# A small store of transposed maxima, issued from ScalarE's queue at some places and from SyncE's at the others

## The chip, the cores and the metric

The program runs on one core of a Trainium2 chip. Its time is the device time of one execution in microseconds (us). Three runs of the kernel before gave 2234.05, 2234.30 and 2235.77 us; the median, 2234.3 us, is the time that the prediction is held against. Beside them one execution was profiled: it took 2233.03 us, and the span of its trace, from the first to the last recorded work, is 2231.2 us. All times inside the trace count from the start of that span.

## The reference

A gated mix of two blocks over the same tokens `x` (2048 tokens of 576 values), in fp32:

```
g   = sigmoid(sum(x * gate_w))                   # one gate a token
q,k,v = split(x @ wqkv), 32 heads of 18 values
p   = softmax(q k^T / sqrt(18))                  # 2048 x 2048 a head
a   = (p v, heads side by side) @ wo
b   = gelu(layernorm(x) @ w1 + b1) @ w2 + b2     # 576 -> 4608 -> 576
out = g * a + (1 - g) * b
```

The softmax needs the maximum of each row of scores. The kernel finds these maxima in a first pass over the scores, and takes them off inside the matmul of a second pass.

## The kernel before

The attention is cut into 32 units: 16 pairs of heads (`pair`), each in two halves of 1024 queries (`unit`, L192). A unit goes through two passes.

First pass (`s1_round`, L220): 32 rounds a unit. In a round TensorE (PE) multiplies 128 queries by 512 keys for both heads (L230), and VectorE (DVE) reduces each 128x512 bank of scores to its 128 maxima (L232). When the last round of a unit is through, `s1_finish` (L234) reduces the four partial maxima, negates them, splits them in a high and a low part (L239 to L241), and transposes the 128x32 result into the tile `tr` (L244). `tr` is then stored to a scratch tensor in DRAM, `mx_scr` (16 KB, L255), and from there two small DMAs put the values as two extra rows for each head into the query tile `qa` of that unit (`rows`, L248; the DMAs are in the helper `dma_r`, L139). The second DMA waits until the store has landed; both are 8 KB.

Second pass (`s2`, L263): for each of 16 key chunks `kc` and two query blocks `qb`, PE multiplies keys by queries with the extra rows included, so that the scores come out with the maxima taken off (L271), ScalarE (ACT) takes the exponential (L274), and PE multiplies by the values (`pv`, L289). The first matmul of a unit's second pass cannot start before both rows of that unit have landed in `qa`. The first pass runs ahead of the second by about one unit.

Between the attention matmuls the kernel weaves in the MLP, piece by piece (`mlp`, L338): `h_pair` (L461) makes two chunks of the hidden layer from the normalised tokens (L490), the gelu runs on ACT (L541, L543) and GpSimd (POOL, `pool_op`, L183), and `out_pair` (L548) multiplies by `w2` (L578) and adds into an accumulator on DVE (L595). The tokens are worked in four blocks of 512. At the end of a block `h_pair` loads the next block's tokens in pieces (`load_y`, L608: `big<-y_scr`, 28 DMAs for a change of block, called from L493 and L494, issued at L139). After the MLP comes the output projection (`out_proj`, L1037; its matmuls are at L1225). Its first input is loaded by `load_o` and `load_den` (L1064, L1076: `x<-ot_scr` and `low<-ot_scr`), while the last unit is still ahead of the second pass.

The order of all this is written out when the program is built. There is a counter of slots, `slot[0]`, raised by `run_due` (L158); `defer(n, fn)` (L146) runs `fn` once n slots have gone by, so that its instructions come at that place in their engine's program. Each engine works its own program in order. DMAs issued from `nc.sync` stand in the program of SyncE (SP) in the order of the calls, and one that waits holds up those behind it. In `s1_finish` the store is deferred by 2 slots and `rows` by 7.

`inflow[0]` holds the slot of the last `load_y` or `load_o`, that is, of the last large load. The two row DMAs already go by GpSimd's queue where the loop has begun (`looped`) and that load is fewer than `BUSY` = 20 slots back, and by SP's elsewhere (L250). The store goes by SP always:

```
queue = nc.gpsimd if looped[0] and slot[0] - inflow[0] < BUSY else nc.sync
...
defer(2, lambda: nc.sync.dma_start(scr, tr))
defer(7, rows)
```

Following the slot counter through the code, the last `load_y` before the store of a unit lies 1 slot back for unit 23 (slots 1493 and 1494), the `load_o` before it lies 1 slot back for unit 31 (2005 and 2006), and for no other unit is a large load fewer than 49 slots back. The store of unit 15 stands one slot ahead of the first `load_y` of its change of block (982 and 983), its `rows` 5 slots later, among those loads.

Of the kernel before, what the change touches and what calls it, by code (L numbers as in the profile page):

```python
# [46 lines left out]
BUSY = 20  # L47
# [22 lines left out]
def gated_mix_kernel(ctx: ExitStack, tc: tile.TileContext, x, wqkv, wo, w1, b1, w2, b2, gate_w, out):  # L70
    nc = tc.nc
# [65 lines left out]
    def dma_r(queue, dst, src):  # L137

        queue.dma_start(dst.bitcast(F32), src)  # L139


    slot = [0]
    inflow = [-BUSY]
    later = []

    def defer(n, fn):  # L146
        later.append((slot[0] + n, fn))
# [86 lines left out]
    def s1_finish(u):  # L234

        m4 = M4.pop(u)
        nm = asm.tile([P, 2, 8], F32, name="nm")
        nm2 = asm.tile([P, 2, 2, 8], F32, name="nm2")
        nc.vector.tensor_reduce(nm, m4, axis=AX.X, op=ALU.max, negate=True)  # L239
        nc.vector.tensor_tensor(nm2[:, :, 0, :].bitcast(F32R), nm, nm, op=ALU.max)  # L240
        nc.vector.tensor_tensor(nm2[:, :, 1, :], nm, nm2[:, :, 0, :], op=ALU.subtract)  # L241

        tr = asm.tile([P, 32], F32, name="tr", bufs=1)
        nc.vector.transpose(tr, nm2.rearrange("p a b c -> p (a b c)"))  # L244

        scr = mx_scr[u % 2]

        def rows():  # L248
            qa = QA[u % 3]
            queue = nc.gpsimd if looped[0] and slot[0] - inflow[0] < BUSY else nc.sync  # L250
            src = scr.rearrange("(i h b t) n -> h b t i n", h=2, b=2, t=8)
            for h in range(2):
                r = 64 * h + 54
                dma_r(queue, qa[r:r + 2, :].rearrange("b (t i n) -> b t i n", i=4, n=32), src[h])
        defer(2, lambda: nc.sync.dma_start(scr, tr))  # L255
        defer(7, rows)

    RING = []
# [69 lines left out]
    looped = [False]  # L328

    def next_round():  # L330
        if rounds:
            u, r = rounds.pop()
            s1_round(u, r)
            if r == NR - 1:
                defer(1, lambda: s1_finish(u))
# [1007 lines left out]
```

## Time and profile before

| | before |
|---|---|
| median of three runs | 2234.3 us |
| the profiled execution | 2233.03 us |
| its span | 2231.2 us |
| PE busy | 2202.0 us, 99% of the span |
| DVE, ACT, POOL busy | 1647.7, 1425.7, 1006.1 us |
| moved by DMA | 329.74 MB, 148 GB/s over the span |
| stores `mx_scr<-tr` at L255, all by SP | 32 of 16 KB |
| row DMAs `qa<-mx_scr` by SP, by POOL | 58 and 6, of 8 KB |

How to read the lines shown below. A row of a timeline is: start, duration (both us), engine, source line, operation, output and input by the program's names, count of instructions merged in the row, and in brackets how long the engine had been idle and what ended that. `SPq`, `ACTq` and `POOLq` are the programs that issue DMAs; a DMA's row there is its issue, not its transfer. A row of the chain of waits, the chain of work that ended last, is: start, duration, and what the chain stood on then; a row such as `DMA mx_scr<-tr` is the time from the issue of that store to its landing, "issue" is time for which the trace shows no cause. In a table of windows the columns are the window, its length, the busy time of PE, PE's weight loads, DVE, ACT and POOL with counts, the clock granted to PE as a share of full speed, the busy share of the DMA engines, and GB/s.

### The profile page before, as it was taken

What the parts mean: (1) busy time and instruction counts of PE and PEld (TensorE: products, weight loads), DVE (VectorE), ACT (ScalarE), POOL (GpSimd) and SP (SyncE); (2) the same over time, 40 slices, a digit from 0 to 9 for tenths busy, and PEclk for the clock granted to TensorE, in tenths of its full rate; (3) what the DMA queues carried; (4) which work ended last, traced back from release to release, by engine and by line L of the source; (5) the groups of instructions that cost most, each with busy time, mean ns of one, the idle gap of its engine ahead of it and who ended that gap; (6) DMA issues with size and microseconds to landing.
All of it is one profiled execution on the core that took longest, in us unless ns stands there. A gap on an engine that the chain in (4) does not pass through costs nothing.

```text
span 2231.2 us, 51473 instructions
## 1 busy us (share of the span) xinstructions
PE 2202.0 (99%) x20496; PEld 1584.4 (71%) x20496; DVE 1647.7 (74%) x2888; ACT 1425.7 (64%) x2623; POOL 1006.1 (45%) x1003
## 2 busy tenths in 40 slices
PE   8999999999999999999999999999989999999989
PEld 7878667677766767767777677776756777776758
DVE  6685777777778777777777777777767777777634
ACT  4333777777776666666666666666656666666662
POOL 4322765666663444444445444444444444444600
PEclk9999999999999999999999999999999999999999
DMA  8867555454464533233354333232634333232354
GB/s 265 269 221 222 189 174 162 146 160 147 157 215 147 161 120 124 100 124 121 120 168 158 106 116 108 100 119 94 181 116 155 119 127 122 100 112 98 114 184 167
DMA packets 171538, 329.74 MB, mean 148 GB/s; under 512 B 65206, under 2 KB 91506, under 8 KB 160570
## 3 DMA queue, kind: packets, MB, share of 16 engines
q1 hardware_dynamic: 169138, 322.70, 44.7%
q8 instruction: 161, 2.64, 0.5%
q10 hardware_dynamic: 1968, 3.70, 0.4%
q14 instruction: 79, 0.65, 0.1%
q0 software_dynamic: 192, 0.06, 0.0%
HBM read 234.00 MB, written 96.69 MB: 148 GB/s over the span
## 4 chain that ended last, share of the span: by engine, by line
PE 94%; DVE 2%; DMA 2%; issue 1%; POOL 1%; ACT 0%; SPq 0%; DVEq 0%; ACTq 0%; POOLq 0%
PE ps L289 21%; PE ps L578 21%; PE ps L490 20%; PE ps L271 13%; PE ps L230 11%; PE ps L890 3%; PE ps L1225 3%; PE ps L911 2%; DVE m L232 1%; DMA mx_scr<-tr 1%; DMA p<-in_A_wqkv_dram 0%; PE ps L766 0%; PE ps L893 0%; PE ps L892 0%; DMA qa<-mx_scr 0%
## 5 line engine op out<-in xcount | busy, mean ns | idle before, releaser
L232 DVE TENSOR_REDUCE m<-ps 128x1 f32<-128x512 f32 x2048 | 1311.0, 684 | 390.4 <-PE ps L230 379.7
L274 ACT ACTIVATE p<-ps 128x512 f32<-128x512 f32 x1048 | 568.6, 596 | 322.5 <-PE ps L271 319.9
L274 ACT ACTIVATE ring<-ps 128x512 f32<-128x512 f32 x1000 | 543.1, 596 | 295.0 <-PE ps L271 293.2
L490 PE MATMUL ps<-big,w 64*128 64x512 f32 x3708 | 570.7, 393 | 0.2 <-issue 0.2
L183 POOL TENSOR_SCALAR zz<-zz 128x512 f32<-128x512 f32 x288 | 178.2, 619 | 736.8 <-ACT zz L543 696.2
L578 PE MATMUL ps<-w,hh 64*128 64x288 f32 x4352 | 478.7, 294 | 1.0 <-DVE x L595 1.0
L271 PE MATMUL ps<-qa,ka 56*128 56x512 f32 x2048 | 451.4, 421 | 16.8 <-DMA qa<-mx_scr 15.8
L578 PEld LDWEIGHTS ps<-w,hh 64*128 64x128 f32 x4352 | 419.1, 187 | 30.6 <-DVE x L595 5.1
L230 PE MATMUL ps<-ka,qa 54*128 54x512 f32 x2048 | 427.6, 398 | 0.1
L490 PEld LDWEIGHTS ps<-big,w 64*128 64x128 f32 x3708 | 371.8, 187 | 64.6 <-issue 0.5
L183 POOL TENSOR_TENSOR zz<-zz,z 128x512 f32<-128x512 f32 x288 | 371.4, 1290 | 24.0
L271 PEld LDWEIGHTS ps<-qa,ka 56*128 56x128 f32 x2048 | 205.7, 184 | 242.8 <-DVE m L232 173.3
L578 PE MATMUL ps<-w,hl 64*128 64x288 f32 x2176 | 340.9, 292 | 0.8 <-POOL hl L183 0.8
L289 PE MATMUL ps<-p,vt 128*32 128x512 f32 x1968 | 239.6, 599 | 0.0
L230 PEld LDWEIGHTS ps<-ka,qa 54*128 54x128 f32 x2048 | 214.8, 185 | 22.3 <-DVE m L232 2.7
L289 PE MATMUL ps<-ring,vt 128*32 128x512 f32 x1872 | 229.5, 603 | 0.0
L578 PEld LDWEIGHTS ps<-w,hl 64*128 64x128 f32 x2176 | 223.4, 185 | 1.2 <-POOL hl L183 1.1
L183 POOL TENSOR_TENSOR hl<-zz,hh 128x512 fp32r<-128x512 f32 x136 | 176.7, 1299 | 11.4
L183 POOL TENSOR_TENSOR w<-x,w 128x576 fp32r<-128x576 f32 (+1 forms) x54 | 98.8, 1841 | 163.9 <-ACT w L394 157.0
L289 PEld LDWEIGHTS ps<-p,vt 128*32 128x32 f32 x1968 | 52.7, 109 | 112.6 <-issue 103.2
L289 PEld LDWEIGHTS ps<-ring,vt 128*32 128x32 f32 x1872 | 50.2, 110 | 107.3 <-issue 107.3
L595 DVE SCALAR_TENSOR_TENSOR x<-ps,x 128x288 f32<-128x288 f32 x256 | 103.6, 446 | 25.9 <-PE ps L578 16.1
(121 smaller groups left out, 1541.7 us busy)
## 6 DMA issues: line engine op xcount, KB each, us to landing
w<-w_scr SPq DMA_DIRECT2D x54, 1152.0 KB
w<-w_scr SPq DMA_DIRECT2D x108, 576.0 KB
x<-in_B_w_dram SPq DMA_DIRECT2D x72, 288.0 KB
w_scr<-w SPq DMA_DIRECT2D x18, 1152.0 KB
w_scr<-w SPq DMA_DIRECT2D x36, 576.0 KB
qa<-qk_scr SPq DMA_DIRECT2D x192, 72.0 KB
ka<-qk_scr SPq DMA_DIRECT2D x84, 144.0 KB
qk_scr<-hh SPq DMA_DIRECT2D x36, 256.0 KB
```

Source lines behind the costliest of these rows:

```text
L183: fn(*args, **kw)
L230: nc.tensor.matmul(ps, qa[r0:r0 + 54, t * P:(t + 1) * P], ka[r0:r0 + 54, kb * TB:(kb + 1) * TB], start=True, stop=True)
L232: nc.vector.tensor_reduce(M4[u][:, h, t, kb:kb + 1], ps, axis=AX.X, op=ALU.max)
L271: nc.tensor.matmul(ps[h], ka[r0:r0 + 56, kc * P:(kc + 1) * P], qa[r0:r0 + 56, qb * TB:(qb + 1) * TB], start=True, stop=True)
L274: nc.scalar.activation(p_of(n)[:, qb, h], ps[h], AF.Exp, scale=SCALE)
L289: nc.tensor.matmul(OB[u][r:r + 32, :], v[:, k, 19 * h:19 * h + 32], p_of(c)[:, qb, h, :], start=(k == 0), stop=(k == NT - 1))
L490: nc.tensor.matmul(ps[h], wt[w_][r, c, :], y[r, c, :], start=(k == 0), stop=(k == 26))
L578: mm = nc.tensor.matmul(ps[nn][:, :ND], h_[r, tok], w_[p_][r, cs[nn]], start=(k == 0), stop=(k == 6 * G - 1))
L595: nc.vector.scalar_tensor_tensor(dst, ps[nn][:, :ND], 0.5, b2b[:, cs[nn]] if g == 0 else dst, op0=ALU.mult, op1=ALU.add)
L890: nc.tensor.matmul(ps, w_[:, c, ms], big[:, s_, :], start=(k == 0), stop=False)
L911: nc.tensor.matmul(ps[:, :ND], big[:, s_, tok], w_[:, c, cs], start=(k == 0), stop=False)
L1225: nc.tensor.matmul(ps[:, :ND], OT[b][2][:, s_, tok], w_part(w_, c)[:, cs], start=(k == 0), stop=(k == 13))
```

## The change

The choice of queue is moved into a helper, `queue_of(aside)`, with the condition unchanged. The rows use it with GpSimd as before. The store uses it with ScalarE: where the last large load is fewer than 20 slots back at the store's own slot, the store is issued from ACT's program, and elsewhere from SP's as before.

```diff
         scr = mx_scr[u % 2]
 
+        def queue_of(aside):
+            return aside if looped[0] and slot[0] - inflow[0] < BUSY else nc.sync
+
         def rows():
             qa = QA[u % 3]
-            queue = nc.gpsimd if looped[0] and slot[0] - inflow[0] < BUSY else nc.sync
+            queue = queue_of(nc.gpsimd)
             src = scr.rearrange("(i h b t) n -> h b t i n", h=2, b=2, t=8)
             for h in range(2):
                 r = 64 * h + 54
                 dma_r(queue, qa[r:r + 2, :].rearrange("b (t i n) -> b t i n", i=4, n=32), src[h])
-        defer(2, lambda: nc.sync.dma_start(scr, tr))
+        defer(2, lambda: queue_of(nc.scalar).dma_start(scr, tr))
         defer(7, rows)
```

## The prediction

> **What bounds the kernel now.** The page first: PE is busy nearly all the span, so whatever holds PE in its program shows in the time, one for one.
>
> ```profile
> PE 2202.0 (99%) x20496; PEld 1584.4 (71%) x20496; DVE 1647.7 (74%) x2888; ACT 1425.7 (64%) x2623; POOL 1006.1 (45%) x1003
> ```
>
> Next the table of waits, for what holds PE by way of a DMA. Of the tensor that the change touches there is one row on PE (in all, times, longest):
>
> ```profile
> PE ps L271 <- DMA qa<-mx_scr: 15.8, 4, 6.4
> ```
>
> Four waits: two row DMAs for each of two units. The chain of waits gives the places. At the first, the first pass of unit 23 is through, and its rows are fetched for its second:
>
> ```profile
> 1620.01 4.50 DMA mx_scr<-tr
> ...
> 1624.90 0.78 POOL qa L139
> ...
> 1627.58 2.54 DMA qa<-mx_scr
> ...
> 1630.25 0.61 PE ps L271
> ...
> 1635.08 0.43 PE ps L271 x2
> ```
>
> The other, for unit 31, the last:
>
> ```profile
> 2115.33 7.51 DMA mx_scr<-tr
> ...
> 2123.23 0.78 POOL qa L139
> ...
> 2125.93 2.33 DMA qa<-mx_scr
> ...
> 2128.39 0.61 PE ps L271
> ...
> 2133.24 0.43 PE ps L271 x2
> ```
>
> Store, landing, two rows by POOL, then PE: at both places this is the path that sets the end. How long the store was late is read from the timelines of DVE (the transpose that makes `tr`) and of SP:
>
> ```profile
> 1607.53 0.21 DVE L244 STREAM_TRANSPOSE tr<-nm 128x32 f32<-128x32 f32 x1 [0.26 <-DVE nm L241]
> 2109.80 0.21 DVE L244 STREAM_TRANSPOSE tr<-nm 128x32 f32<-128x32 f32 x1
> ```
>
> ```profile
> 1605.87 14.05 SPq L139 DMA_DIRECT2D big<-y_scr  x20
> 2111.27 0.37 SPq L1069 DMA_DIRECT2D x<-ot_scr  x1
> ```
>
> `tr` was there at 1607.74, but SP was issuing twenty pieces of the next block until 1619.92: the store left 12.3 us late. In unit 31 `tr` was there at 2110.01; SP issued the loads of the projection first, from 2111.27, and the store at 2115.33, 5.3 us late, to land behind them after 7.51.
>
> **Which stores move.** By the slot counter, units 23 and 31. Unit 15's rows go by POOL, but its store does not move, and SP's timeline shows it ahead of its loads:
>
> ```profile
> 1122.83 0.33 SPq L255 DMA_DIRECT2D mx_scr<-tr  x1
> 1124.63 5.78 SPq L139 DMA_DIRECT2D big<-y_scr  x8
> ```
>
> So two DMAs change queue; the order of everything else stays, since the slot counter does not look at the queue.
>
> **What the two stalls cost.** I set the work that stood behind each stall beside the same work without one. At the first, PE's last unhindered stretch and pieces of the chain just before:
>
> ```profile
> 1620.44 0.45 PE L578 MATMUL ps<-w,hh 64*128 64x288 f32 x4
> ```
>
> ```profile
> 1613.48 0.40 PE ps L578 x6
> 1613.88 0.23 PE ps L271 x2
> ...
> 1614.51 0.24 PE ps L230 x2
> 1614.75 1.85 PE ps L289 x16
> ```
>
> That stretch takes 0.40, so the first matmul of the second pass was due at 1620.84. Then come two L271, six L578, two L230 and sixteen L289: 0.23 + 0.40 + 0.24 + 1.85 = 2.72, to 1623.56. The trace is there at 1635.08: 11.5 us lost. Of these the wait is 1630.25 - 1620.84 = 9.4; the other 2.1 are the same instructions run slower after it, with this clock (the column ahead of the DMA share, 0.50):
>
> ```profile
> 1625.00:1630.00 5.00, 0.76 (x1) 0.28 (x1) 0.00 (x0) 0.60 (x1) 3.02 (x4) 0.50 0.07 4
> ```
>
> At the second:
>
> ```profile
> 2119.90 0.44 PE L578 MATMUL ps<-w,w 64*128 64x288 f32 x4
> ```
>
> ```profile
> 2136.80 0.26 PE ps L271 x2
> 2137.05 0.52 PE ps L578 x8
> 2137.58 2.01 PE ps L289 x16
> ```
>
> Four L578 take half of 0.52, so the rows were due at 2120.17; 0.26 + 0.52 + 2.01 = 2.79 leads to 2122.96, against 2133.24: 10.3 us lost (8.2 of waiting, 2.1 of slow clock). Together 21.8 us, the most that the change can give.
>
> **What the moved store costs on ACT.** ACT takes two issues more; SP has two fewer, and nothing on SP waited for these. By the order of the code the store of unit 23 stands in ACT's program behind the activation at L511, that of unit 31 ahead of an exponential at 2110.50:
>
> ```profile
> 1607.50 0.69 ACT L511 ACTIVATE z<-ps,b1t 128x512 f32<-128x512 f32 x1
> 2110.50 1.09 ACT L274 ACTIVATE p<-ps 128x512 f32<-128x512 f32 x2 [1.60 <-PE ps L271]
> 2190.19 0.37 ACTq L1236 DMA_DIRECT2D out_dram<-res  x1
> 2190.79 0.63 ACT L1141 ACTIVATE big<-x 128x512 fp32r<-128x512 f32 x1 [1.23 <-DVE x L1138]
> ```
>
> ACT reaches the first at about 1608.2, after `tr` (1607.74): no wait. It reaches the second in a gap in which it idled 1.60 us for PE anyway, and waits there for `tr` until 2110.01. Behind the waiting store are the exponentials, on which PE's banks depend. An issue on ACT takes 0.37 us in the row shown, so the exponential at 2110.50 is held by 0 to 0.3 us; an issue slowed like SP's own in these stretches (14.05 / 20 = 0.70) holds it 0.3 more. ACT is busy 64%, and I charge 0.2 us for both stores, with bounds of 0 and 1.
>
> **When the rows land then.** Landing of such a store with nothing around it, by a unit whose rows SP itself issues once it has landed:
>
> ```profile
> 1182.97 0.32 SPq L255 DMA_DIRECT2D mx_scr<-tr  x1
> ...
> 1184.43 1.32 SPq L139 DMA_DIRECT2D qa<-mx_scr  x2
> ```
>
> 1.46 us; the worst row is the 7.51 above. On ACT's queue beside large loads no row exists, so these are the bounds. POOL's program and its row DMAs, the last two and the landing from unit 15, whose rows went out among loads:
>
> ```profile
> 1611.94 1.29 POOL L183 TENSOR_TENSOR zz<-zz,z 128x512 f32<-128x512 f32 x1
> 2109.82 1.42 POOL L1051 TENSOR_TENSOR wlast<-x,big 128x576 fp32r<-128x576 f32 x1
> 1124.97 0.90 POOL L139 DMA_DIRECT2D qa<-mx_scr  x1 [2.72 <-DMA mx_scr<-tr]
> 1128.32 0.74 POOL L139 DMA_DIRECT2D qa<-mx_scr  x1 [2.45 <-issue]
> DMA to landing us min/median/max: 3.0/3.2/3.3
> ```
>
> The pair takes 3.35 + 3.2 = 6.55 us among loads (5.2 and 5.0 at the two stalls, where the loads were over). Unit 23: POOL is free at 1613.23; the store, issued about 1608.3, has landed by 1609.8, or by 1612.8 with the 4.50 of its own stretch. Rows at 1613.23 + 6.55 = 1619.8, due at 1620.84: no stall, 1.1 us to spare. With 7.51: 1615.8 + 0.4 (POOL's reaction, 2122.84 to 2123.23) + 6.55 = 1622.8, a stall of 1.9. Unit 31: the store leaves at 2110.1, ahead of the loads instead of behind them; landed by 2111.6, rows by 2112.0 + 6.55 = 2118.5, due at 2120.17: 1.6 to spare. With 7.51: 2117.6 + 0.4 + 6.55 = 2124.5, a stall of 4.4. I take no stall at either, nearest to the quiet row, since neither store then has a large load ahead of it on its own queue, and charge 0.3 us for the small spare.
>
> The Trainium skill speaks against this in "DMA: Bandwidth & Descriptors", section "Issuing engines are not separate DMA queues": transfers issued from different engines end on the same 16 DMA engines and interleave, and another issuing engine saves issue time alone. By that rule the waits for SP's turn (12.3 and 5.3 us) go, the landing of 4.50 and 7.51 stays; unit 23 would be free all the same, unit 31 would keep some stall. That is the second case below, priced there from rows.
>
> **What is late next.** Behind the rows POOL's gelu steps move forward as PE does. SP behind the old stores only waits for PE and POOL. The next block's pieces have left SP by 1619.92, and PE turns to them after 1623.6, first piece first. In unit 31 DVE stands at
>
> ```profile
> 2121.72 0.69 DVE L1138 TENSOR_TENSOR x<-x,low 128x512 f32<-128x512 f32 x1 [5.96 <-DMA low<-ot_scr]
> ```
>
> until 2122.41, with the accumulations that free PE's banks behind it, and PE now asks for a bank from 2122.96 on: 0.3 us charged, 0 to 1 possible. From there to the end the chain stands on PE or on DVE steps that follow PE, so the gain is kept.
>
> **Sum.** 11.5 + 10.3 - 0.2 - 0.3 - 0.3 = 21.0 us. The profiled execution would go from 2233.03 to 2212.0; the median lies 1.3 above it, so the forecast is 2234.3 - 21.0 = 2213.3 us.
>
> **The rivals.**
>
> Slow landing or slow rows under load, chance 0.13. The store lands after 7.51 at both, the rows at unit 15's pace: stalls of 1.9 and 4.4, with up to 1 us of slow clock: 21.8 - 6.3 - 1 = 14.5 to 18.5 saved, 2216 to 2220. For it: the saturated loads. Against: unit 15's rows, on a queue of their own, landed in 3.0 to 3.3 among loads.
>
> One stall only goes, chance 0.10: the rows of one unit wait until its loads have drained, or PE is held by a piece or bank not there yet. 10.3 to 11.5 saved: 2223 to 2224. Against: the dues above have 1.1 and 1.6 us to spare.
>
> It doesn't do what it says, 0.04: the stores wait for the loads on any queue, and the rows land when they did: 2234.
>
> Slower, 0.03: ACT's program is held until its store has landed, and this lands when it did before. Place: behind L511 and ahead of 2110.50. ACT stands from 1608.2 to 1624.51 and from 2110.05 to 2122.84: 29.1 us, less 1.6 idle, plus 4.2 of slow clock, where 21.8 were lost: 9.9 slower, 2244. It decides once the two holds together pass about 19 us (21.8 + 1.6 - 4.2). Against: at 2190.19 ACT issues a store of 288 KB and works again at 2190.79.
>
> **How the numbers follow.** The forecast has 0.70, its own range 2211 to 2216. Adding the second case and the edge of the third gives 2210.5 to 2223, with under 2 in 10 left out. 0.2% is 4.5 us, about what a measurement of this kernel tells from no change: faster 0.93 (the first three), same 0.04, slower 0.03.
>
> **What would show it.** After: no wait of L271 on `qa<-mx_scr`; two `mx_scr<-tr` in ACT's program at about 1608 and 2110, 30 in SP's; POOL's rows near 1613 and 2112; no window at clock 0.50 around them; the second-pass matmuls of these units at about 1621, and at 2120 less the 11.5 gained before. It is wrong if ACT's exponentials wait at the stores, if the stores still land near 1624, or if PE loses the time again before its last projection.

## The result, and the profile after

| | before | after |
|---|---|---|
| median | 2234.17 us (6 runs) | 2218.23 us (6 runs, 2217.93 to 2222.36) |
| profiled execution | 2233.03 us | 2218.35 us |
| its span | 2231.2 us | 2216.6 us |

The ratio is 0.9933, 95% interval 0.992 to 0.9946: 15.9 us faster. The forecast was 2213.3 us, 21.0 faster; the time lies inside the whole range (2210.5 to 2223) and outside the forecast's own narrower one (2211 to 2216). The stores moved and landed early as predicted, but a part of the stalls stayed.

Line numbers after L250 are three higher in the changed kernel (L271 is now L274, L289 is L292). The waits of PE on a row DMA, in all, times, longest:

```profile
PE ps L274 <- DMA qa<-mx_scr: 4.4, 2, 2.5
```

15.8 us in four waits have become 4.4 in two. The timeline of ACT has the two moved stores, each of them right behind its transpose, and the exponential behind the second waits for PE as long as before (1.59 for 1.60):

```profile
1607.34 0.35 ACTq L258 DMA_DIRECT2D mx_scr<-tr  x1
...
2100.50 0.33 ACTq L258 DMA_DIRECT2D mx_scr<-tr  x1
2100.94 1.09 ACT L277 ACTIVATE p<-ps 128x512 f32<-128x512 f32 x2 [1.59 <-PE ps L274]
```

The chain of waits at unit 23, and at unit 31:

```profile
1617.93 4.55 DMA qa<-mx_scr
...
1622.62 0.41 PE ps L274
...
1625.58 0.42 PE ps L274 x2
...
2100.50 1.42 DMA mx_scr<-tr
...
2102.31 0.78 POOL qa L139
2103.09 6.01 issue
2109.10 4.35 DMA qa<-mx_scr
...
2117.99 0.43 PE ps L274 x2
```

The store of unit 31 lands in 1.42 us where it took 7.51. But the chain still runs over the rows: between POOL's two row DMAs lie 6.01 us for which the chain finds no cause. The timeline of PE shows which row is late:

```profile
1620.34 0.40 PE L274 MATMUL ps<-qa,ka 56*128 56x512 f32 x1
1622.62 0.47 PE L274 MATMUL ps<-qa,ka 56*128 56x512 f32 x1 [1.89 <-DMA qa<-mx_scr]
...
2110.64 0.40 PE L274 MATMUL ps<-qa,ka 56*128 56x512 f32 x1
2113.58 0.76 PE L274 MATMUL ps<-qa,ka 56*128 56x512 f32 x1 [2.54 <-DMA qa<-mx_scr]
```

At both places the first head's row is there in time, and the second head's is not.

Where the time went, by work that both traces have (the transposes of units 23 and 31 and the end of the last DVE step; of before, only the last has not been shown). After, then before:

```profile
1607.02 0.21 DVE L244 STREAM_TRANSPOSE tr<-nm 128x32 f32<-128x32 f32 x1 [0.26 <-DVE nm L241]
2100.26 0.21 DVE L244 STREAM_TRANSPOSE tr<-nm 128x32 f32<-128x32 f32 x1
...
2212.70 0.52 DVE L1232 SCALAR_TENSOR_TENSOR res<-ps,gate,bt 128x288 f32<-128x288 f32 x1 [1.34 <-PE ps L1228]
```

```profile
2227.38 0.52 DVE L1229 SCALAR_TENSOR_TENSOR res<-ps,gate,bt 128x288 f32<-128x288 f32 x1 [1.34 <-PE ps L1225]
```

Up to the first transpose the traces differ by 0.5 us. Unit 23: PE's row of 1635.08 is now at 1625.58, 9.5 earlier, less 0.5: 9.0 gained of 11.5. Unit 31: 2133.24 is now 2117.99, 15.25 earlier, and the transpose before it was 9.54 earlier: 5.7 gained of 10.3. From there to the end 0.6 is given back (14.7 earlier at the last step). 0.5 + 9.0 + 5.7 - 0.6 = 14.6 us, the difference of the spans.

### The profile page after: what moved, and what is told of

Its sections match the earlier page's. It is cut to its first block, busy times and chain, and to the rows that moved or that the text cites. A ratio compares the mean times of both kernels' runs of the same rounds, so it can differ in the third digit from the quotient of the medians.

```text
span 2216.6 us, 51478 instructions
## 1 busy us (share of the span) xinstructions
PE 2199.0 (99%) x20496; PEld 1581.8 (71%) x20496; DVE 1647.5 (74%) x2888; ACT 1426.5 (64%) x2623; POOL 1006.1 (45%) x1003
## 4 chain that ended last, share of the span: by engine, by line
PE 93%; DMA 2%; DVE 2%; issue 1%; POOL 1%; ACT 0%; SPq 0%; DVEq 0%; ACTq 0%; POOLq 0%
PE ps L292 21%; PE ps L581 20%; PE ps L493 20%; PE ps L274 13%; PE ps L230 11%; PE ps L893 3%; PE ps L1228 2%; PE ps L914 2%; DVE m L232 1%; DMA p<-in_A_wqkv_dram 0%; DMA big<-y_scr 0%; DMA qa<-mx_scr 0%; PE ps L769 0%; DMA out_dram<-res 0%; PE ps L895 0%
## 5 line engine op out<-in xcount | busy, mean ns | idle before, releaser
L274 PE MATMUL ps<-qa,ka 56*128 56x512 f32 x2048 | 448.9, 420 | 5.4 <-DMA qa<-mx_scr 4.4
L274 PEld LDWEIGHTS ps<-qa,ka 56*128 56x128 f32 x2048 | 204.7, 184 | 230.5 <-DVE m L232 174.2
L292 PE MATMUL ps<-p,vt 128*32 128x512 f32 x1968 | 239.2, 598 | 0.0
L292 PE MATMUL ps<-ring,vt 128*32 128x512 f32 x1872 | 228.4, 600 | 0.0
L292 PEld LDWEIGHTS ps<-p,vt 128*32 128x32 f32 x1968 | 52.6, 109 | 112.6 <-issue 103.3
L292 PEld LDWEIGHTS ps<-ring,vt 128*32 128x32 f32 x1872 | 49.9, 109 | 106.6 <-issue 106.6
L598 DVE SCALAR_TENSOR_TENSOR x<-ps,x 128x288 f32<-128x288 f32 x256 | 103.6, 447 | 12.4 <-PE ps L581 10.3
```

What stands on the lines that cost most here:

```text
L274: nc.tensor.matmul(ps[h], ka[r0:r0 + 56, kc * P:(kc + 1) * P], qa[r0:r0 + 56, qb * TB:(qb + 1) * TB], start=True, stop=True)
L292: nc.tensor.matmul(OB[u][r:r + 32, :], v[:, k, 19 * h:19 * h + 32], p_of(c)[:, qb, h, :], start=(k == 0), stop=(k == NT - 1))
L598: nc.vector.scalar_tensor_tensor(dst, ps[nn][:, :ND], 0.5, b2b[:, cs[nn]] if g == 0 else dst, op0=ALU.mult, op1=ALU.add)
```

## The experiments

The theory formed from the trace after is about GpSimd's pair of row DMAs. Its timeline at unit 23, and for both units the least, median and greatest time from a row's issue to its landing:

```profile
1612.68 0.78 POOL L139 DMA_DIRECT2D qa<-mx_scr  x1
1617.93 0.74 POOL L139 DMA_DIRECT2D qa<-mx_scr  x1 [4.47 <-issue]
```

```profile
DMA to landing us min/median/max: 4.6/4.7/4.9
DMA to landing us min/median/max: 4.3/5.4/6.5
```

The second landed 4.55 us after its issue, so the 4.9 is the first's: it landed at 1617.6, and the second was issued at 1617.93. At unit 31 the first landed 6.5 after 2102.31, at 2108.8, and the second was issued at 2109.10. The trace of before has the same pattern, overlooked in the prediction: at unit 15 the first row landed 3.0 after its issue (the 3.3 is the second's), 1124.97 + 3.0 = 1127.97, and the second row's issue is at 1128.32. At all three places the issue follows the landing by about 0.3 us. So the theory: POOL cannot issue the second row until the first has landed, because the room for its DMA descriptors, set to 1024 bytes where the program is built, does not take both. The rival: POOL is slow at issuing while large loads run.

### More room for GpSimd's descriptors, in the changed kernel

```diff
-    nc = _bacc.Bacc(..., dynamic_dma_scratch_size=1024)
+    nc = _bacc.Bacc(..., dynamic_dma_scratch_size=1152)
...
-        nm = asm.tile([P, 2, 8], F32, name="nm")
-        nm2 = asm.tile([P, 2, 2, 8], F32, name="nm2")
+        nm = asm.tile([P, 2, 8], F32, name="nm", bufs=1)
+        nm2 = asm.tile([P, 2, 2, 8], F32, name="nm2", bufs=1)
```

> The changed kernel with more room for GpSimd's DMA descriptors (1152 bytes where it has 1024; nm and nm2 get one buffer for two to make the space). Theory: the second row DMA is late because POOL can issue it only when the first has landed, for want of room. Then the second is issued within 1 us of the first, at about 1613.5 and 2103.1; with the landings of the trace after (4.9 and 6.5) both rows are there by 1618.4 and 2109.6, ahead of the dues 1620.3 and 2110.7; PE has no wait on the rows, 2.5 + 4.5 = 7.0 us go, about 2211 us. Rival: POOL is slow to issue among large loads, whatever its room: the second row starts 5.2 and 6.8 us behind the first as now, about 2218 us.

Measured: 2214.02 us (4 runs, 2213.37 to 2214.31); ratio to before 0.9911 (0.9897 to 0.9926). POOL's rows, and landings at units 23 and 31:

```profile
1613.80 1.55 POOL L139 DMA_DIRECT2D qa<-mx_scr  x2
...
2101.40 1.56 POOL L139 DMA_DIRECT2D qa<-mx_scr  x2 [0.58 <-DMA mx_scr<-tr]
```

```profile
DMA to landing us min/median/max: 5.8/6.2/6.5
DMA to landing us min/median/max: 6.5/6.6/6.7
```

Both rows go out in one run of 1.55 us, and no wait of PE on a row is left in the trace. The theory holds and the rival falls. With both in flight at once the rows took 5.8 to 6.7 us to land, where the expectation took 4.9 and 6.5, and were yet in time. To make the space the edit also leaves two small tiles one buffer for two; that alone was not run, but DVE alone writes and reads these tiles. In PE's timeline the first matmuls of both second passes go through in pairs without a wait, and a new, small wait follows at unit 31:

```profile
1621.47 0.41 PE L274 MATMUL ps<-qa,ka 56*128 56x512 f32 x2
...
2109.70 0.39 PE L274 MATMUL ps<-qa,ka 56*128 56x512 f32 x2
...
2113.72 0.89 PE L581 MATMUL ps<-w,hh 64*128 64x288 f32 x4 [0.82 <-DVE x L598]
```

It is the wait that the prediction charged with 0.3 us, 0 to 1 possible: DVE's accumulations stand behind the step that waits for the load of `low`.

```profile
2112.61 0.69 DVE L1141 TENSOR_TENSOR x<-x,low 128x512 f32<-128x512 f32 x1 [7.28 <-DMA low<-ot_scr]
```

4.2 us of the 7.0 expected show in the medians (3.6 if each is set against the kernel before measured beside it). The trace says where they are, by the same work as above: the transposes stand at 1608.14 and 2099.34, the row of 1635.08 at 1624.38, the one that PE's timeline of before has at 2133.16 at 2112.41, and the last step at 2208.60. So 11.3 of the 11.5 us are gained at unit 23 and 10.3 of the 10.3 at unit 31: the stalls are gone. Against that, this execution reached unit 23 0.6 us later than before did (1.1 later than after), and from unit 31 to the end 2.0 us are given back, where after gave back 0.6. The wait of 0.82 and the slower matmuls behind it (0.89 for four, 0.43 before the gap) are part of these 2.0; the rest was not followed. It is the fastest version measured here.

### The same room in the kernel before

> The kernel before with the same added room. Theory: the second row follows the first within 1 us at both stalls where it took 2.7; PE's second wait (2.08 and 1.88 us) falls under 0.5 each, about 2230.5 to 2231.5 us. Rival (the issue itself is slow): spacing 2.7 as before, about 2234 us.

Measured: 2231.23 us (10 runs, 2229.86 to 2233.11), ratio 0.9991 (0.9982 to 1.0001). The trace is plain where the time alone is not:

```profile
1626.51 1.55 POOL L139 DMA_DIRECT2D qa<-mx_scr  x2 [12.51 <-DMA mx_scr<-tr]
...
2122.52 1.55 POOL L139 DMA_DIRECT2D qa<-mx_scr  x2 [11.71 <-DMA mx_scr<-tr]
```

```profile
1629.88 0.76 PE L271 MATMUL ps<-qa,ka 56*128 56x512 f32 x1 [0.17 <-DMA qa<-mx_scr]
...
2125.06 1.67 PE L271 MATMUL ps<-qa,ka 56*128 56x512 f32 x2 [5.22 <-DMA qa<-mx_scr]
```

The second waits, 2.08 and 1.88 before, are 0.17 and none. So at these two places too, where the landings were fast (2.3 to 2.5 us), the second row had waited for the first one's landing.

### The rows on ScalarE's queue too

```diff
-            queue = queue_of(nc.gpsimd)
+            queue = queue_of(nc.scalar if u != 15 else nc.gpsimd)
```

> The changed kernel, with the two row DMAs of units 23 and 31 on ACT's queue too. Theory: issued on ACT at about 1612.2 and 2105.2, one behind the other; landed 3 to 6.5 us later, by 1618.5 and 2108.5 to 2111.8; no wait at the first, 0 to 1.2 us at the second, ACT held for about 1.3 us at each: 2211 to 2213 us. Rival: small transfers among large loads land late on every queue and ACT's hold costs PE: 2215 to 2219 us.

Measured: 2215.86 us (4 runs, 2215.44 to 2216.17), ratio 0.992 (0.9905 to 0.9935): above the 2211 to 2213 of the theory, in the rival's stretch. PE does not wait for a row any more, but ACT does for its own second issue at unit 31 (ACT's timeline, then PE's):

```profile
2102.65 0.66 ACTq L139 DMA_DIRECT2D qa<-mx_scr  x1
...
2106.43 0.60 ACTq L139 DMA_DIRECT2D qa<-mx_scr  x1
2107.08 1.09 ACT L277 ACTIVATE p<-ps 128x512 f32<-128x512 f32 x2 [3.46 <-DMA x<-ot_scr]
```

```profile
2107.73 1.53 PE L292 MATMUL ps<-p,vt 128*32 128x512 f32 x4 [1.51 <-ACT p L277]
```

The exponentials stood 3.46 us behind the second row's issue, and PE lost 1.51 us waiting for them. Here ACT was held, which the prediction's slower case feared for the store: not by the store, but between two row DMAs among large loads. What held the issue for 3.1 us is open; the chain puts it down to the load of `x`.

### The store on ScalarE's queue, but behind the loads

```diff
-        defer(2, lambda: queue_of(nc.scalar).dma_start(scr, tr))
+        defer(5 if u == 31 else 2, lambda: queue_of(nc.scalar).dma_start(scr, tr))
```

> The changed kernel with unit 31's store on ACT three slots later, so that SP has issued the loads ahead of it. If ACT's queue of its own spares the store the large loads, it lands in 1.5 to 3.5 us, POOL's first row starts at about 2108, and the time is 2219 to 2222 us. If the store only landed fast (1.42 us) because it went out ahead of the loads, it now takes 5 us or more, the rows start at about 2110 or later, and the time is 2222 to 2225 us.

Measured: 2221.71 us (one run). SP's timeline, then the chain:

```profile
2103.19 1.98 SPq L1075 DMA_DIRECT2D x<-ot_scr  x2
2105.21 0.59 SPq L1097 DMA_DIRECT2D low<-ot_scr  x1
```

```profile
2104.52 5.64 DMA mx_scr<-tr
...
2110.55 0.78 POOL qa L139
```

The store was issued at 2104.52: behind the load of `x`, but still ahead of that of `low`, so the edit put it behind half of the large loads and not behind all. On a queue of its own it took 5.64 us to land even so, nearer to the 7.51 on SP's queue than to the 1.42 of the change. The landing and the start of the rows (2110.55) are those of the second outcome that was expected; the time, 0.3 us under its range and within that of the first, does not tell the two apart. So at unit 31 most of the faster landing came from going out ahead of the loads, as far as one run shows.

### One store alone

```diff
-        defer(2, lambda: queue_of(nc.scalar).dma_start(scr, tr))
+        defer(2, lambda: (queue_of(nc.scalar) if u == 23 else nc.sync).dma_start(scr, tr))
```

> Of the changed kernel only unit 23's store goes by ACT, unit 31's by SP as before. If the two gains add as the trace after has them (11.5 - 2.5 = 9.0 us at unit 23, 10.3 - 4.5 = 5.8 at unit 31), this is 9 us faster than before, about 2225 us. Rival: part of unit 23's gain is only passed on to unit 31 and lost there, 4 to 7 us faster.

> Of the changed kernel only unit 31's store goes by ACT. By the sum of the two gains 5.8 us faster than before, about 2228 us; by the rival, up to 11 us faster.

(The other kernel has 31 in the place of 23.) Measured: unit 23 alone 2223.59 us, ratio 0.9956 (0.9942 to 0.9971), 10.1 us under before (2233.67 us, measured beside it); unit 31 alone 2228.56 us, ratio 0.9976 (0.9967 to 0.9986), 5.1 us under it. PE's waits on rows in the one and in the other:

```profile
PE ps L274 <- DMA qa<-mx_scr: 8.9, 3, 5.4
```

```profile
PE ps L274 <- DMA qa<-mx_scr: 11.1, 3, 7.1
```

The place whose store moved has one wait left, of 1.5 us (unit 23) and 2.1 us (unit 31), the second row's; the other place keeps both. Within the spread of the runs (4.4 us between the ten of unit 31 alone) nothing is handed on from one place to the other.

### The changed kernel again

> The changed kernel again, beside the others of this call: 2217.5 to 2219.5 us; the two single gains (9 and 5.8 us) add up to its own, 14.8 to 16, if they are independent.

Measured: 2218.11 us (4 runs, 2215.17 to 2220.90), ratio 0.9932 (0.9918 to 0.9947), 15.6 us under before. The single gains make 15.2.

Its profiled execution took 2215.17 us, 3.2 less than the one of the trace after, and shows how far one trace of this kernel may be from another. PE's timeline, then a window behind the second wait in the trace after and in this one (the clock stands ahead of the DMA share):

```profile
1621.18 0.47 PE L274 MATMUL ps<-qa,ka 56*128 56x512 f32 x1 [0.32 <-DMA qa<-mx_scr]
...
2112.26 0.47 PE L274 MATMUL ps<-qa,ka 56*128 56x512 f32 x1 [2.63 <-DMA qa<-mx_scr]
```

```profile
2112.50:2115.00 2.50, 1.42 (x9) 1.40 (x9) 0.69 (x1) 0.62 (x2) 0.00 (x0) 0.71 0.16 53
```

```profile
2112.50:2115.00 2.50, 2.50 (x25) 0.94 (x23) 0.82 (x2) 1.11 (x2) 0.74 (x1) 1.00 0.03 7
```

At unit 23 the first row landed after 3.6 us for 4.9, the second was issued 0.3 us later again, and PE waited 0.32 us for 1.89. At unit 31 the wait was as long as before (2.63 for 2.54 us), but the clock stayed at 1.00 where it had fallen to 0.71. By the work used above 10.6 of 11.5 us were gained here at unit 23 and 7.2 of 10.3 at unit 31, for 9.0 and 5.7. So what a trace gives for the two places differed by about 1.5 us each between these two executions.

### Unit 31's store by SyncE, ahead of the loads

```diff
-        defer(2, lambda: queue_of(nc.scalar).dma_start(scr, tr))
+        defer(1 if u == 31 else 2, lambda: (nc.sync if u == 31 else queue_of(nc.scalar)).dma_start(scr, tr))
```

> Unit 23's store by ACT as changed; unit 31's by SP, but one slot earlier, ahead of the loads in SP's program. Theory: what counted at unit 31 was to go out ahead of the loads, not the queue: it is issued at about 2100.5 and lands in 1.4 to 2 us as on ACT, POOL's rows start near 2102.3, and the time is that of the changed kernel, 2217 to 2219 us. Rival: ACT's own queue sped the landing; then 3 us or more of landing and 2219 to 2222 us.

Measured: 2218.68 us (4 runs, 2216.94 to 2221.70), ratio 0.9933 (0.9916 to 0.9949). SP's timeline, then the chain; this trace runs 2.5 us later than the one after:

```profile
2103.03 0.32 SPq L258 DMA_DIRECT2D mx_scr<-tr  x1
2104.27 0.38 SPq L1072 DMA_DIRECT2D x<-ot_scr  x1
```

```profile
2103.03 1.40 DMA mx_scr<-tr
...
2104.83 0.78 POOL qa L139
2105.61 6.35 issue
```

The store lands in 1.40 us from SP's queue as it does in 1.42 from ACT's, and the time is that of the changed kernel within the spread of its runs. At unit 31 the order counts and the queue does not. At unit 23 the store becomes ready in the midst of a run of issues on SP, so there another queue is what lets it go first; an SP order that does the same was not tried.

## Why the prediction was right, and where not

**The bound, the stores that move, the price of the stalls: right.** The four waits on the rows were the path. Two stores moved, at 1607.34 and 2100.50, where about 1608 and 2110 were named; the second is earlier by what was gained at the first place. With both rows on time (the kernel with more room) 11.3 and 10.3 us were gained at the two places, and 11.5 and 10.3 had been read for them: the stalls were priced right.

**The cost on ACT: right.** The exponential behind the second store idles 1.59 us for PE as before. The hold that the slower case feared did not come at either store.

**The store's landing: right value at unit 31, for a reason that was half right.** 1.42 us was measured there for the 1.46 taken. At unit 23 the trace shows only that it had landed when POOL came free at 1612.68, 5.3 us after its issue. The prediction's reason was that no large load stood ahead of the store on its own queue. That was so in the kernel with the store behind the load of `x` as well, and there the landing took 5.64 us. What counted was that the store went out ahead of the loads on all queues: in the window from 2100.0 to 2102.5 the DMA engines' share was 0.04. The Trainium skill's rule, in "DMA: Bandwidth & Descriptors", section "Issuing engines are not separate DMA queues", is that another issuing engine saves issue time alone, since all transfers share 16 DMA engines. The 5.64 us on ACT's queue agree with it. But the earlier issue at unit 31 also met nearly idle DMA engines, so the landing fell too, and did not stay at 7.51 as the second case had it.

**The step that failed: "The pair takes 3.35 + 3.2 = 6.55 us among loads".** It was 5.25 + 4.55 = 9.8 us at unit 23 and 6.79 + 4.35 = 11.1 at unit 31, so the spare of 1.1 and 1.6 us turned into waits of 1.9 and 2.5, the second with a slow clock behind it (0.71 in the window shown above): 11.5 - 9.0 = 2.5 and 10.3 - 5.7 = 4.6 us lost, against the 0.3 charged for this step. In the second trace of the same kernel the pair took 8.2 and 11.2 us. Two errors lie in it. The 3.35 was taken for a price of issuing; it is the first row's landing, so a slow landing counts twice. And unit 15 was taken as "among loads", though its rows went out as the loads began. Windows of before at unit 15 (DMA share 0.51, ahead of the GB/s), then of after at units 23 and 31:

```profile
1125.00:1130.00 5.00, 5.00 (x46) 4.08 (x44) 2.80 (x5) 2.50 (x5) 1.61 (x2) 1.00 0.51 135
```

```profile
1615.00:1617.50 2.50, 2.50 (x30) 1.53 (x24) 1.52 (x4) 1.17 (x3) 0.00 (x0) 1.00 1.05 182
...
2107.50:2110.00 2.50, 2.50 (x38) 2.39 (x36) 0.00 (x0) 1.49 (x3) 0.90 (x2) 1.00 0.98 343
```

With the DMA engines full, a row took 4.3 to 6.5 us in this trace (3.6 to 6.8 over all runs) where it took 3.0 to 3.3 there. That the time lies inside the whole range is in part luck. The second case had the right outcome (14.5 to 18.5 saved, 2216 to 2220), but for the wrong part of the path: it made the store slow and kept the rows at unit 15's pace. Nor does its sum lead to the 18.5: 21.8 - 6.3 less up to 1 is 14.5 to 15.5. It was given 0.13.

**What is late next: right in place, too small.** The wait for the accumulations stayed covered after the change and showed with 0.82 us as soon as the rows were on time, for the 0.3 charged. That the rest of the gain is kept to the end was off: 0.6 us were given back after the change, and 2.0 with the rows on time.

## What to carry to other kernels

A stall's price is read well from the same work without it; what remains of the stall must be priced under the load that the earlier start puts it in, not under that of the nearest row. Where two small DMAs follow each other on GpSimd, set the second one's issue beside the first one's landing: if they coincide at several places, the room for descriptors is the cause to try first, and 128 bytes more removed it here. In these runs a small transfer that others wait for did best ahead of the large loads, and which queue it took mattered only where its own was in the midst of issuing them. And one trace is one execution: a second trace of the same kernel had other waits and another clock.

## What the runs showed of the hardware

Not expected: in the kernels with 1024 bytes of room, GpSimd's second row DMA was issued about 0.3 us after the first had landed, wherever POOL issued the two (5.25 and 6.79 us behind the first under full load), and with 1152 bytes both went out within 1.7 us. The landing of an 8 KB row rose from 2.3 to 2.6 us, with the loads over, to 3.6 to 6.8 where the DMA share was near 1 most of the time. The same 16 KB store took 1.4 us ahead of 2.6 MB of loads on either queue, and 5.64 behind the first half of them on a queue of its own (one run). ACT was held for 3.1 us between two row DMAs among these loads, for a cause that stays open. After a wait of PE of 2.54 us the granted clock fell to 0.71, and after one of 2.63 us, in another execution of the same kernel, it stayed at 1.00.
